# A Conformer block on one core: token tiles of 127 rows in place of 125

## Chip, core and metric

The kernel runs on 1 core of one Trainium2 chip. The metric is the device time of one execution in microseconds (us), the median of several runs. The profile is of one execution; its span runs from the first to the last instruction and is 3.8 to 4.3 us shorter than the time of the same run. All runs told here are in the fast state, with a mean granted TensorE clock of 0.998 to 1.000 of full speed.

## The reference, cut to what matters

Two batches of 4000 tokens with 512 features; a feed-forward, full attention inside each batch, a convolution block, a second feed-forward.

```python
B, T, D, K = (2, 4000, 512, 3);  F = 4 * D
h = _silu(layernorm(x) @ w_ff1_a) @ w_ff1_b              # FF1
x1 = x + 0.5 * h
q, k, v = (layernorm(x1) @ w for w in (w_q, w_k, w_v))
p = softmax(q @ k.T * scale)                             # 4000 x 4000 for each batch
x2 = x1 + (p @ v) @ w_o
a, b = split(layernorm(x2) @ w_pw1)                      # pointwise product 1
h = a * sigmoid(b);  dc = depthwise_conv(h, dw)          # 3 taps along the tokens
h = _silu(batchnorm(dc)) @ w_pw2                         # pointwise product 2
x3 = x2 + h
h = _silu(layernorm(x3) @ w_ff2_a) @ w_ff2_b             # FF2
return layernorm(x3 + 0.5 * h)
```

## The kernel before

Tokens sit in tiles of 125 rows, 64 tiles for 8000 tokens, and are worked on in 16 chunks of 4 tiles, 500 tokens:

```python
TILE = 125
CHUNK = 500
TPC = CHUNK // TILE
NT = N // TILE           # 64
NCK = N // CHUNK         # 16 chunks
TCB = T // CHUNK         # 8 chunks of a batch
KT = -(-T // 128)        # 32 key tiles of a batch
```

In the first half of a feed-forward the weights are the stationary operand and the tokens stream; in the second half a token tile is stationary and 512 features stream, whatever the number of its rows:

```python
def ff_first(self, c, f, p, b_p):
    ...
    for cc in range(0 if done else DC):
        self.mm(out, self.Wa[:, cc, f * 128:(f + 1) * 128], self.lnT[c % 2][:, :, cc, 0:TILE], ...)
    self.act(p, ps[:, 0:CHUNK], AF.Silu, [b_ps], [b_p])

def ff_second(self, f, ti, p, b_p, inc):
    self.mm(self.Yb[ti][0:TILE, :], p[:, ti * TILE:(ti + 1) * TILE], self.Wb[:, f, :], ...)
```

Attention takes one chunk of queries `g` after the other, and in it 32 key blocks `kt` (4 score and 4 value matmuls each). Beside the blocks, other work is put in: queries of the next chunk are fetched (blocks 7 to 10) and multiplied (14 to 20), the pointwise product of the chunk before runs (`pair`, at blocks 22 and 27), and in chunk 7 the keys of batch 1 replace those of batch 0, one key tile for each block from block 6 on:

```python
if g + 1 < NCK and 7 <= kt < 7 + TPC:
    self.fetch_queries((g + 1) // TCB, (g + 1) % TCB, kt - 7)
if g + 1 < NCK and kt in (14, 16, 18, 20):
    self.q_group((g + 1) // TCB, (g + 1) % TCB, (kt - 14) // 2)
if not self.any_score:
    if g == TCB - 1 and kt >= 6:
        self.key_tile(1, kt - 6)
    if g == TCB and kt < 6:
        self.key_tile(1, KT - 6 + kt)
hook(g, kt)              # kt 22, 27: pair(g - 1, ...); kt 3, 8: pair(g - 2, ...)
```

A key tile is two transfers, and both are issued by SyncE (SP), which also issues all the other transposes, stores and loads of this stage (the times are those of SP's timeline in the profile before, at 952.93 and 953.56 us):

```python
def key_tile(self, b, kt):
    ...
    self.load(self.h[kt], src, [self.b_h[kt]], reads=rd)                 # on SP: 0.58 us of its queue
    self.transpose(self.hT[kc][:, kj], src, rd, [self.b_hT[kc][kj]])     # on SP: 1.19 us of its queue
```

SP's timeline shows its transfers one after the other, none begun before the one ahead was done (from 930.13 to 962.67 us, 32.54 us, in the profile before), so what stands behind a key tile in SP's order waits for it.

## Time and profile before

| | kernel before |
|---|---|
| time, median of 3 (lowest to highest) | 2054.76 us (2054.47 to 2054.98) |
| span of the profiled run | 2050.2 us |
| TensorE (PE) busy | 2037.8 us, 99% |
| VectorE (DVE), ScalarE (ACT), GpSimd (POOL) busy | 54%, 36%, 5% |
| second halves of the feed-forwards | 2016 matmuls of 125 rows x 512 columns |

The lines behind the table stand in the prediction. PE is the bound and has next to no gaps, so only two things move the time: fewer or shorter matmuls, and waits of PE. In the list of waits of the SP queue in the stretch of attention chunk 7 (from 928 to 968 us; columns: who waits, for whom, us in all, times, longest) the first row is:

```profile
SPq L529 <- DVE wff L1030: 3.3, 1, 3.3
```

SP (its queue is shown as SPq) stood still once for 3.3 us, for a piece of the convolution on VectorE whose result it stores. The store began at 930.13 us, when VectorE was done, and what stands behind it from 930.49 on; neither was set by TensorE.

### The profile page before, as it was taken

The page shows a single profiled execution, that of the slowest core. Times are in us where ns is not written, and L with a number is a line of the kernel's source. Part 1 is how long each engine was busy: PE and PEld are TensorE (multiplying, and loading weights), DVE is VectorE, ACT ScalarE, POOL GpSimd, SP SyncE. Part 2 cuts the span into 40 slices and gives each one's busy share as a digit, 9 for nine tenths or more (in the row PEclk, how much of TensorE's full clock was granted, in tenths as well). Part 3 has the DMA queues.
Part 4 walks back from the last instruction along what each step waited for, and adds up shares of the span by engine and source line. Part 5 has one row for each costly group of instructions (what it writes and reads, how often), then busy time and mean ns, then how long its engine had stood idle before and what let it go on. Part 6 is the DMA issues. An engine that isn't in the chain of part 4 may idle for free.

```text
span 2050.2 us, 24503 instructions
## 1 busy us (share of the span) xinstructions
PE 2037.8 (99%) x9653; PEld 1031.8 (50%) x9653; DVE 1099.0 (54%) x2274; ACT 742.7 (36%) x1270; POOL 112.2 (5%) x241
## 2 busy tenths in 40 slices
PE   9999999999999999999999999999999999999998
PEld 5555555554444444444444444444445555555554
DVE  4234444325556667666666676667764543543443
ACT  3433333333333333333333333333345343443432
POOL 1000000000000000000000000000011000000000
PEclk9999999999999999999999999999999999999999
DMA  7122256420101111115411110111143111111111
GB/s 184 51 61 61 53 103 125 90 69 16 26 16 30 25 29 26 34 23 116 107 27 24 29 34 24 24 29 34 47 120 93 31 34 39 31 33 39 31 31 42
DMA packets 253417, 104.60 MB, mean 51 GB/s; under 512 B 193703, under 2 KB 252784, under 8 KB 253296
## 3 DMA queue, kind: packets, MB, share of 16 engines
q1 hardware_dynamic: 252900, 102.65, 21.4%
q8 instruction: 78, 1.28, 0.3%
q14 instruction: 43, 0.35, 0.1%
q10 hardware_dynamic: 396, 0.31, 0.0%
HBM read 33.73 MB, written 23.31 MB: 28 GB/s over the span
## 4 chain that ended last, share of the span: by engine, by line
PE 98%; DVE 1%; POOL 0%; issue 0%; ACT 0%; DMA 0%; POOLq 0%; SPq 0%; DVEq 0%; ACTq 0%
PE s L470 55%; PE y L470 42%; DVE work L552 0%; POOL work L672 0%; DVE work L574 0%; DVE wff L1092 0%; DVE xt L695 0%; DMA xt<-in_x_dram 0%; DVE work L509 0%; POOL work L1101 0%; DVE work L665 0%; ACT work L512 0%; DVE wff L997 0%; DVE work L618 0%; DVE work L670 0%
## 5 line engine op out<-in xcount | busy, mean ns | idle before, releaser
L512 ACT ACTIVATE work<-s 128x500 bf16<-128x500 f32 (+1 forms) x1060 | 621.6, 587 | 1218.0 <-PE s L470 1216.6
L470 PE MATMUL s<-work,wff 128*128 128x500 bf16 (+2 forms) x2592 | 628.5, 373 | 1.9 <-DVE work L509 1.7
L470 PE MATMUL s<-work,keys 128*128 128x500 bf16 x2048 | 517.5, 374 | 0.1
L470 PE MATMUL y<-wff,work 128*125 128x512 bf16 x2016 | 506.6, 379 | 0.0
L470 PE MATMUL y<-work,keys 128*128 128x500 bf16 (+1 forms) x2048 | 504.6, 374 | 0.4 <-DVE work L929 0.4
L854 DVE TENSOR_TENSOR work<-work 128x500 f32<-128x500 f32 (+1 forms) x496 | 334.4, 674 | 280.0 <-ACT work L512 277.2
L470 PEld LDWEIGHTS s<-work,wff 128*128 128x128 bf16 x2592 | 250.6, 98 | 279.8 <-issue 5.8
L470 PEld LDWEIGHTS y<-wff,work 128*125 128x125 bf16 x2016 | 275.2, 137 | 173.5
L470 PEld LDWEIGHTS s<-work,keys 128*128 128x128 bf16 x2048 | 199.8, 98 | 232.2 <-DVE work L778 0.6
L470 PEld LDWEIGHTS y<-work,keys 128*128 128x128 bf16 (+1 forms) x2048 | 194.6, 97 | 234.0 <-issue 6.2
L695 DVE SCALAR_TENSOR_TENSOR xt<-y,xt 125x512 bf16<-125x512 f32 x128 | 79.8, 683 | 353.0 <-PE y L470 353.0
L552 DVE BATCH_NORM_STATS2 work<-xt 125x6 f32<-125x512 bf16 x316 | 199.7, 680 | 8.3 <-DMA xt<-in_x_dram 8.1
L470 PE MATMUL s<-work 128*125 128x512 bf16 (+2 forms) x780 | 197.7, 378 | 2.0 <-DVE work L1202 1.2
L561 POOL TENSOR_TENSOR work<-work 125x4 f32<-125x4 f32 x76 | 77.0, 1013 | 1131.5 <-DVE work L559 1131.5
L470 PEld LDWEIGHTS s<-work 128*125 128x125 bf16 (+1 forms) x780 | 95.3, 124 | 76.9 <-issue 3.7
L574 DVE TENSOR_SCALAR work<-xt,work 125x512 bf16<-125x512 bf16 x311 | 113.9, 412 | 26.3 <-POOL work L561 22.5
L695 DVE SCALAR_TENSOR_TENSOR xt<-s,xt 125x512 bf16<-125x512 f32 x56 | 38.7, 691 | 146.4 <-PE s L470 146.4
L695 DVE SCALAR_TENSOR_TENSOR xt<-s,work,xt 125x512 bf16<-125x512 f32 x64 | 48.0, 751 | 32.2 <-PE s L470 31.5
L1001 DVE SCALAR_TENSOR_TENSOR wff<-wff,s 128x500 bf16<-128x500 f32 x57 | 38.5, 676 | 40.8 <-PE s L470 40.8
L512 ACT ACTIVATE wff<-s 128x500 f32<-128x500 f32 x67 | 39.5, 591 | 54.8 <-PE s L470 54.8
L512 ACT ACTIVATE work<-keys,work 128x500 bf16<-128x500 bf16 x64 | 50.5, 796 | 1.1 <-DVE work L1106 1.1
L1071 POOL COPY wff<-wff 128x1 bf16<-128x1 bf16 x56 | 10.5, 187 | 635.4 <-DVE wff L1001 633.0
(83 smaller groups left out, 429.6 us busy)
## 6 DMA issues: line engine op xcount, KB each, us to landing
keys<-keysd SPq DMA_DIRECT2D x62, 128.0 KB, 2.3
xt<-in_x_dram SPq DMA_DIRECT2D x15, 500.0 KB
out_dram<-work SPq DMA_DIRECT2D x15, 500.0 KB
dcvd<-wff SPq DMA_DIRECT2D x52, 125.0 KB, 1.7
keys<-dcvd SPq DMA_DIRECT2D x13, 500.0 KB, 5.1
keysd<-work SPq DMA_DIRECT2D x16, 320.0 KB, 3.2
wff<-in_w_ff_a_dram SPq DMA_DIRECT2D x16, 256.0 KB, 3.9
work<-work SPq DMA_TRANSPOSE x210, 2.5
```

What stands on the lines that cost most here:

```text
L470: self.S.op("PE", lambda e: e.matmul(out, lhsT, rhs, start=start, stop=stop, **kw), reads=reads, writes=[bank], inc=stop if inc is None el ...
L512: return self.S.op("ACT", lambda e: e.activation(out, in_, func, **kw), reads=reads, writes=writes)
L552: self.S.op("DVE", lambda e: e.bn_stats(self.st[sl][:, ti, :], x), reads=[b_x], writes=[self.b_st[sl][ti]])
L561: S.op("POOL", lambda e: e.tensor_tensor(out=self.rs[sl], in0=self.va[sl], in1=self.neghalf[0:TILE, :], op=ALU.pow), reads=self.b_va[sl] + ...
L574: self.S.op("DVE", lambda e: e.tensor_scalar(out, x, self.mv[sl][:, ti, 0:1], self.rs[sl][:, ti:ti + 1], ALU.subtract, ALU.mult), reads=[b ...
L695: self.S.op("DVE", lambda e: e.scalar_tensor_tensor(out=self.XT[g], in0=ps, scalar=scalar, in1=self.XT[g], op0=ALU.mult, op1=ALU.add), rea ...
L854: S.op("DVE", lambda e, p=p, n=n, acc=acc: e.tensor_tensor(out=acc, in0=acc, in1=self.P[p][0:n], op=ALU.add), reads=[self.b_P[p], self.b_a ...
L1001: self.S.op("DVE", lambda e: e.scalar_tensor_tensor(out=out, in0=self.th[k], scalar=1.0, in1=ps[:, 0:CHUNK], op0=ALU.add, op1=ALU.mult), r ...
L1071: S.op("POOL", lambda e: e.tensor_copy(self.G[gs][:, jj, 0:1], self.G[gp][:, jj, CHUNK:CHUNK + 1]), reads=[self.b_G[gp][jj]], writes=[self ...
```

## The change

The intent is to fill the tiles better: 4000 = 31 x 127 + 63, so a batch takes 31 full tiles and a rest of 63 tokens. The rests of both batches share one tile (rows 0 to 62 and 64 to 126). That is 63 tiles in place of 64. A chunk has 508 tokens, the last one of each batch 444, of which the last 63 are in the shared tile.

```diff
-TILE = 125
-CHUNK = 500
-TPC = CHUNK // TILE
-NT = N // TILE
-NCK = N // CHUNK
-TCB = T // CHUNK
+TILE = 127
+TPC = 4
+CHUNK = TPC * TILE
+TCB = -(-T // CHUNK)
+NCK = B * TCB
+TAIL = T % TILE
+NT = NCK * TPC - 1
+SHARED = TCB * TPC - 1
+HALF = 64
...
+def width(c):
+    return CHUNK if c % TCB < TCB - 1 else T - (TCB - 1) * CHUNK      # 508, or 444
+def token_tiles(c):
+    return TPC if c < NCK - 1 else TPC - 1
+def tile_at(c, ti):
+    return SHARED if c == NCK - 1 and ti == TPC - 1 else c * TPC + ti
...
-    ROWS = ((0, 80), (80, TILE))
+    ROWS = ((0, 112), (112, TILE))
...
 # ff_first, ff_second: n = token_tiles(c) tiles, the last chunk has 3
-                for ti in range(TPC):
-                    self.ff_second(f, ti, self.P[s], self.b_P[s], f == FC - 1 or ti == TPC - 1)
+                n = token_tiles(c)
+                for ti in range(n):
+                    self.ff_second(f, ti, self.P[s], self.b_P[s], f == FC - 1 or ti == n - 1)
...
 # attention: chunks of width W
-                    self.mm(ps[:, 0:CHUNK], self.hT[kc][:, kj, cc, :], self.qT[s][:, cc, :],
+                    self.mm(ps[:, 0:W], self.hT[kc][:, kj, cc, :], self.qT[s][:, cc, 0:W],
...
 # pointwise product 1: the short chunk of batch 0 in two pieces, 381 and 63 columns
+            if n < TPC:
+                moves.append((ps[:, n * TILE:W], self.lnT[0][:, n, :, tile_rows(t, n)]))
...
 # loads and stores of a chunk in pieces of 112 and 15 rows (load_x before: one transfer of 125 rows)
+            res += [(rows[r0:r1], tiles[r0:r1, lo:min(hi, n), :]) for r0, r1 in self.ROWS]
```

The order of the instructions on the SP queue and the blocks to which key tiles, queries and pointwise products are tied stay as they were.

## The prediction

A weight load took 98 ns with 128 columns and 137 with 125, both less than the 211 and 216 ns from one matmul to the next. The "2.4" in the sums is the step from 211 to 216 ns over 12 columns, 2.4 columns for each ns.

> **What bounds the kernel now.** I read the page's busy times and its chain first, then the groups of matmuls by form, then timelines of one feed-forward and one attention stretch, and last the DMA-issuing queue (SPq) in attention chunk 7. From the page:
>
> ```profile
> span 2050.2 us, 24503 instructions
> ...
> PE 2037.8 (99%) x9653; PEld 1031.8 (50%) x9653; DVE 1099.0 (54%) x2274; ACT 742.7 (36%) x1270; POOL 112.2 (5%) x241
> ...
> PE 98%; DVE 1%; POOL 0%; issue 0%; ACT 0%; DMA 0%; POOLq 0%; SPq 0%; DVEq 0%; ACTq 0%
> ```
>
> TensorE is busy for all but 12.4 us of the span, and the chain that ended last is 98% matmuls. No other engine is above 54%. So the time is the sum of matmul pitches (start to next start), plus 12.4 us of gaps: about 2.8 us in the head, 3.5 where attention ends, 5.5 after the last matmul. A changed instruction on DVE, ACT or POOL is worth nothing except there. The groups, one row for each form:
>
> ```profile
> L470 PE MATMUL y<-wff,work 128*125 128x512 bf16 x2016 | 506.6, 379 | 0.0
> ...
> L470 PEld LDWEIGHTS s<-work,wff 128*128 128x128 bf16 x2592 | 250.6, 98 | 279.8 <-issue 5.8
> L470 PEld LDWEIGHTS y<-wff,work 128*125 128x125 bf16 x2016 | 275.2, 137 | 173.5
> ```
>
> The first row is the second half of both feed-forwards: a token tile of 125 rows is the stationary operand, 512 features stream past. Its length is 512 whatever the tile's rows. The mean of 379 ns is a latency, not a pitch (2016 x 379 exceeds the group's busy time), so the pitch is read from starts, in the timeline of PE:
>
> ```profile
> 218.56 1.89 PE L470 MATMUL y<-wff,work 128*125 128x512 bf16 x8
> 220.29 1.01 PE L470 MATMUL s<-work,wff 128*128 128x500 bf16 x4
> ...
> 831.91 1.00 PE L470 MATMUL y<-work,keys 128*128 128x500 bf16 x4
> 832.75 1.01 PE L470 MATMUL s<-work,keys 128*128 128x500 bf16 x4
> 833.60 1.00 PE L470 MATMUL y<-work,keys 128*128 128x500 bf16 x4
> ```
>
> Eight of 512 columns take 220.29 - 218.56 = 1.73 us, 216 ns each. Eight of 500 take 833.60 - 831.91 = 1.69 us, 211 ns each. A matmul is paid by the columns it streams, about 0.4 ns each, plus about 3 ns.
>
> [...]
>
> **The change part by part.** I counted matmuls and streamed columns of both built programs (the part that runs): 9652 and 4,816,721 before, 9648 and 4,798,121 after.
>
> Removed: one token tile of 64. Each feed-forward loses 16 matmuls of 512 columns, the second pointwise product 4. That is 36 x 216 ns = 7.8 us, all on PE, so all on the path.
>
> Unchanged: the first halves of the feed-forwards, scores, values, queries and first pointwise product stream the same 4000 tokens per batch. Matmuls of 508 cost 3.3 ns more than those of 500, those of 444 and 381 (last chunk of a batch) less; the sum of columns there differs by only -168, below 0.1 us. The projections stay at 64 groups of 4, because a shared tile is projected once for each batch.
>
> Added on PE: for chunk 7 each group of the first pointwise product is split into 381 + 63 columns: 8 groups x 4 = 32 more matmuls of 63 columns with a full weight load. In the head, 16 matmuls of 125 columns start at 7.92 us and the next work at 9.00, or 68 ns each, and 16 weight loads of 128x128 take 0.92 us, or 57 ns each. I take 57 ns for a 63-column one. The pair 381 + 63 then costs 162 + 57 = 219 ns against 188 in one piece: 31 ns x 32 = 1.0 us.
>
> Moved, and the part where I had to choose: attention chunks 7 and 15 are only 444 wide. A key block (4 score and 4 value matmuls) falls from 1.69 to 1.69 - 8 x 56 / 2.4 ns = 1.50 us. In chunk 7 of the kernel before, the SP queue brings in the other batch's keys, and it is full:
>
> ```profile
> 952.93 0.58 SPq L516 DMA_DIRECT2D keys<-keysd  x1
> 953.56 1.19 SPq L520 DMA_TRANSPOSE keys<-keysd  x1
> 954.85 3.33 SPq L520 DMA_TRANSPOSE work<-work  x2
> 958.23 0.57 SPq L516 DMA_DIRECT2D keys<-keysd  x1
> 958.86 1.20 SPq L520 DMA_TRANSPOSE keys<-keysd  x1
> 960.15 2.52 SPq L520 DMA_TRANSPOSE work<-work  x2
> ```
>
> One key tile costs the queue 0.58 + 1.19 us and two gaps, 1.85 us, and behind them stand the four transposes that the pointwise product at key block 22 reads. The last is issued at about 961.4 and lands about 2.6 us later, at 964.0. The chain shows the product there with a small wait of its own, against the same place one chunk earlier:
>
> ```profile
> 896.88 2.55 PE s L470 x12
> ...
> 964.22 2.62 PE s L470 x12
> ```
>
> Slack there is nil (0.07 us waited). Afterwards PE arrives 22 x 0.187 = 4.1 us earlier, less 0.1 for the 508-wide pieces between. The queue's 32.5 us from 930.13 to 962.67 do not shrink: it starts when a store of about block 7 is ready, 7 x 0.187 = 1.3 us earlier, and one gap of 0.4 us (947.22 to 947.60) can close. PE then waits 0.07 + 4.0 - 1.7 = 2.4 us; I take 2.2. Nothing gives this back, as PE is the bound. In chunk 15 the transposes for block 22 are issued from 1491.35, the last at 1496.0 with 2.9 us to landing, so 1498.9, and PE needs them at 1499.53: 0.6 us of slack. The 5.5 blocks from the normalisation to there shrink by 1.0 us: a wait of about 0.5 us.
>
> Where attention ends, a chain of VectorE work runs, part of it on the last chunk, now 444 wide in place of 500. Four gates and four statistics of 0.68 us lose about 0.07 us each: 0.4 us less, allowing for two split copies.
>
> Sum: -7.8 + 1.0 + 2.2 + 0.5 - 0.4 = -4.5 us. On 2054.76 that is 2050.3 us, 0.2% faster.
>
> **Rivals.** (1) The full gain: the SP queue speeds up with PE, because what gates it are key tiles released by PE, and no wait appears. For it: the wait list of that stretch shows a few SPq waits on PE. Against: from 947.60 on the queue's pieces stand nearly end to end. Then -7.8 + 1.0 - 0.4 = -7.2: 2047.6 us. (2) A larger wait: the transposes are slowed further by the queue's long pieces (one took 2.03 us in place of 1.2), or the next query fetch in chunk 8 is late too (its slack before is about 1.9 us, after about 0.7 to 1.5), or chunk 15, where VectorE is 78% busy, becomes bound by VectorE for a few blocks. Then waits of 5 to 6 us eat most of the gain: 2053 us. (3) The transfers of 112 + 15 rows or the doubled count of issues hurt head or end. Against: outside attention SP is mostly idle, and head and end move one tile each as before; at most 0.3 us either way. (4) A weight load of 127 columns shows at the 381-wide matmuls of the short chunk (162 ns): 137 ns still fits; at most some tenths.
>
> **Range and chances.** The 7.8 us are nearly certain, the 1.0 within 0.5 us; the waits of 2.7 us may be 0 to 6. Runs before lie within 0.5 us. So 2050.3, with 2047.6 to 2052.8 for 8 in 10. A change of 2% is 41 us, far outside all of it: faster by over 2% 0.005, within 2% 0.985, slower by over 2% 0.01.
>
> **What would show it.** Groups: 1992 + 24 matmuls of 127 rows with 512 columns, each still at 216 ns pitch, weight loads at about 137 ns. A feed-forward chunk at 27.4 us before should be about 27.6 (508 wide), and the last about 20.9. The 63-column pieces at about 57 ns. PE idle for about 2 us just before block 22 of chunk 7, released by a DMA transpose, with SPq full before it, and about 0.5 us in chunk 15. Wrong would be: PE's pitch of 508 above 215 ns, no idle in chunk 7 (then rival 1), idle of more than 4 us there, or a gap at a new place.

## The result, and the profile after

| | before | after |
|---|---|---|
| time, median (lowest to highest) | 2054.61 us (2054.38 to 2054.98), 4 runs | 2053.22 us (2051.23 to 2054.26), 4 runs |
| ratio of the fast runs, 95% interval | | 0.9992 (0.9975 to 1.0009) |
| span of the profiled run | 2050.2 us | 2047.4 us |

A ratio here is the mean time of one kernel's fast runs over that of the other's of the same rounds, so it is not quite the ratio of the medians beside it. The prediction of 2050.3 us was 2.9 us too low, and the result lies 0.4 us above the range. Two things stand out: the gain is 1.4 us at the median in place of 4.5, and the runs spread over 3.0 us where those before spread over 0.6. The profiled run of the changed kernel is its fastest one (2051.23 us), so its profile alone cannot explain the median.

From the page after, the span, the busy times and the chain:

```profile
span 2047.4 us, 24513 instructions
...
PE 2029.9 (99%) x9647; PEld 1028.7 (50%) x9649; DVE 1092.7 (53%) x2264; ACT 744.9 (36%) x1274; POOL 109.7 (5%) x236
...
PE 97%; DVE 1%; DMA 0%; SPq 0%; issue 0%; POOL 0%; ACT 0%; POOLq 0%; DVEq 0%; ACTq 0%
```

PE is busy for 2037.8 - 2029.9 = 7.9 us less, but the span is only 2.8 us shorter: some 5 us came back as waits of PE. DMA and SPq now stand ahead of issue in the chain. The groups (line, engine, operation, operands, partitions x elements, count; busy us, mean ns; idle before) show the change itself:

```profile
L500 PE MATMUL y<-wff,work 128*127 128x512 bf16 x1992 | 501.2, 379 | 0.0
...
L500 PEld LDWEIGHTS y<-wff,work 128*127 128x127 bf16 x1992 | 273.7, 137 | 171.4
```

There are 24 fewer matmuls in this group, at the same latency, and a weight load of 127 columns takes 137 ns as one of 125 did. Where the time went is seen by stages. The limits were read from both chains of work and PE timelines (times from the span's start):

| stage | before, us | after, us | difference |
|---|---|---|---|
| head, up to the first second-half matmul | 14.11 | 14.51 | +0.40 |
| FF1, up to the first query product | 440.05 | 436.97 | -3.08 |
| attention | 1064.98 | 1068.97 | +3.99 |
| transition to FF2 | 38.48 | 38.48 | 0.00 |
| FF2, up to its last tile | 483.68 | 479.36 | -4.32 |
| end | 8.9 | 9.1 | +0.2 |

The feed-forwards give what they should (another 0.4 us of FF1's share falls after the first query product, and so into attention). Attention takes nearly all of it back, and most of that at one place. From the timeline of PE after (start, us, instructions, the idle time before them and what ended it):

```profile
962.56 0.91 PE L500 MATMUL y<-work,keys 128*128 128x444 bf16 x4
966.97 1.89 PE L500 MATMUL s<-work,wff 128*128 128x508 bf16 x8 [3.50 <-issue]
```

These eight are the pointwise product at key block 22 of chunk 7, the place the prediction named. "issue" hides the cause: the last semaphore event that the profile shows was long past when PE started. The chain through this stretch (start, us, what) shows what PE followed:

```profile
963.03 2.44 DMA work<-work
965.47 1.50 issue
966.97 2.64 PE s L500 x12
```

A transpose into the operand (`work<-work`) began at 963.03 and was done after 2.44 us; another transpose was issued right behind it, and PE started 1.50 us after the first had landed. The SP queue's timeline shows those two and what they stood behind:

```profile
958.18 2.89 SPq L558 DMA_TRANSPOSE work<-work  x2
961.12 0.57 SPq L554 DMA_DIRECT2D keys<-keysd  x1
961.74 1.19 SPq L558 DMA_TRANSPOSE keys<-keysd  x1
963.03 2.52 SPq L558 DMA_TRANSPOSE work<-work  x2
```

The transposes that PE needs are issued at 958.18 and 963.03, without a pause, with a key tile's two transfers between them. SP was done with the last at 965.55; before, it was done at 962.67. PE reached block 22 at 964.07 then and at 963.31 now. And as before, this queue was let go by VectorE:

```profile
SPq L567 <- DVE wff L1112: 3.2, 1, 3.2
```

The wait of 3.5 us explains the profiled run. A second profile of the same kernel, below, explains a part of the spread.

### The profile page after: what moved, and what is told of

Its sections match the earlier page's. It is cut to its first block, busy times and chain, and to the rows that moved or that the text cites. A ratio compares the mean times of both kernels' runs of the same rounds, so it can differ in the third digit from the quotient of the medians.

```text
span 2047.4 us, 24513 instructions
## 1 busy us (share of the span) xinstructions
PE 2029.9 (99%) x9647; PEld 1028.7 (50%) x9649; DVE 1092.7 (53%) x2264; ACT 744.9 (36%) x1274; POOL 109.7 (5%) x236
## 4 chain that ended last, share of the span: by engine, by line
PE 97%; DVE 1%; DMA 0%; SPq 0%; issue 0%; POOL 0%; ACT 0%; POOLq 0%; DVEq 0%; ACTq 0%
PE s L500 55%; PE y L500 42%; DVE wff L1176 0%; SPq L558 0%; DVE work L612 0%; DMA work<-work 0%; DMA wff<-in_w_ff_a_dram 0%; DVE xt L753 0%; SPq L562 0%; DVE work L634 0%; POOL work L726 0%; POOL work L1185 0%; ACT work L550 0%; DVE work L547 0%; SPq L554 0%
## 5 line engine op out<-in xcount | busy, mean ns | idle before, releaser
L550 ACT ACTIVATE work<-s 128x508 bf16<-128x508 f32 (+3 forms) x1060 | 622.8, 588 | 1211.9 <-PE s L500 1208.3
L500 PE MATMUL s<-work,wff 128*128 128x508 bf16 (+5 forms) x2624 | 628.3, 371 | 6.4 <-issue 3.5
L500 PE MATMUL s<-work,keys 128*128 128x508 bf16 (+1 forms) x2048 | 516.8, 374 | 0.1
L500 PE MATMUL y<-work,keys 128*128 128x508 bf16 (+2 forms) x2048 | 504.2, 373 | 0.4 <-DVE work L999 0.4
L500 PE MATMUL y<-wff,work 128*127 128x512 bf16 x1992 | 501.2, 379 | 0.0
L920 DVE TENSOR_TENSOR work<-work 128x508 f32<-128x508 f32 (+2 forms) x496 | 334.5, 674 | 279.8 <-ACT work L550 278.6
L500 PEld LDWEIGHTS y<-wff,work 128*127 128x127 bf16 x1992 | 273.7, 137 | 171.4
L612 DVE BATCH_NORM_STATS2 work<-xt 127x6 f32<-127x512 bf16 x312 | 197.2, 680 | 5.9 <-DMA xt<-in_x_dram 5.8
L500 PE MATMUL s<-work 128*127 128x512 bf16 (+3 forms) x776 | 197.0, 378 | 2.2 <-DVE work L1292 1.2
L634 DVE TENSOR_SCALAR work<-xt,work 127x512 bf16<-127x512 bf16 x307 | 110.7, 406 | 26.2 <-POOL work L621 23.0
```

Of the source, the lines that this page charges most:

```text
L500: self.S.op("PE", lambda e: e.matmul(out, lhsT, rhs, start=start, stop=stop, **kw), reads=reads, writes=[bank], inc=stop if inc is None el ...
L550: return self.S.op("ACT", lambda e: e.activation(out, in_, func, **kw), reads=reads, writes=writes)
L612: self.S.op("DVE", lambda e: e.bn_stats(self.st[sl][:, ti, :], x), reads=[b_x], writes=[self.b_st[sl][ti]])
L634: self.S.op("DVE", lambda e: e.tensor_scalar(out, x, self.mv[sl][:, ti, 0:1], self.rs[sl][:, ti:ti + 1], ALU.subtract, ALU.mult), reads=[b ...
L920: S.op("DVE", lambda e, p=p, n=n, acc=acc: e.tensor_tensor(out=acc, in0=acc, in1=self.P[p][0:n, 0:W], op=ALU.add), reads=[self.b_P[p], sel ...
```

## The experiments

Two theories stood against each other. The clock theory (A in the texts): the gain is lost in the wait before block 22, and in the slower runs a second time, because the wait lets TensorE's granted clock fall. The rival: the wait costs what it lasts, and the spread comes from elsewhere (a wait whose length varies, the pieces of the transfers, the head). All kernels ran with 5 rounds beside the kernel before on the same chip, and all gave the right result. The medians of the kernel before were 2054.45 us (2054.09 to 2055.09) on the chip of the first batch, 2054.32 (2053.58 to 2055.87) on that of the second and 2054.49 (2054.30 to 2056.72) on that of the third; the mean clocks told are those of the records. These are nine runs each, so the kernel before itself spreads over 1.0, 2.3 and 2.4 us, more than the 0.6 of the four runs above.

### e0_after: the changed kernel again

No edit.

> The changed kernel again, to see its spread and the span and clock of each run. Theory A[...]: the runs spread over 2051 to 2054.5 us, and longer runs show a lower mean granted clock. Rival B (the spread was the state of that chip, nothing of the kernel): on this chip the runs lie within 0.6 us as those of the kernel before do, near 2051.2.

Measured: 2053.25 us (2051.70 to 2054.03), ratio 0.9991 (0.9978 to 1.0005). The profile fell on a run of 2053.85 us and shows what the first did not. From PE's timeline:

```profile
966.81 3.55 PE L500 MATMUL s<-work,wff 128*128 128x508 bf16 x8 [3.81 <-issue]
```

The same eight matmuls take 3.55 us in place of 1.89. The table of stretches (us, then busy time of PE, PEld, DVE, ACT, POOL, then the granted clock PEclk, DMA share, GB/s) has the reason, first in the fast profile of the changed kernel, then in this one:

```profile
963.00:967.00 4.00, 0.50 (x4) 0.09 (x3) 0.62 (x1) 0.30 (x1) 0.00 (x0) 1.00 0.50 102
967.00:970.00 3.00, 3.00 (x15) 1.43 (x16) 0.69 (x1) 0.95 (x2) 0.28 (x2) 1.00 0.64 156
```

```profile
963.00:967.00 4.00, 0.19 (x1) 0.14 (x2) 0.48 (x1) 0.00 (x0) 0.00 (x0) 0.80 0.53 111
967.00:970.00 3.00, 3.00 (x8) 1.04 (x7) 0.00 (x0) 0.59 (x1) 0.00 (x0) 0.50 0.63 157
970.00:974.00 4.00, 4.00 (x16) 1.77 (x15) 1.31 (x2) 0.90 (x2) 0.30 (x2) 0.72 0.54 132
```

PEclk is the third number from the right: 1.00 throughout in the one, 0.80, 0.50 and 0.72 in the other, with 8 matmuls in 3 us in place of 15. From the start of the product, 16 matmuls take 972.69 - 966.81 = 5.88 us here and 970.19 - 966.97 = 3.22 in the fast profile: the drop costs 2.66 us more. The two spans, 2050.0 and 2047.4 us, differ by 2.6. So one part of the spread is this: about the same wait, with or without a clock drop after it. The first four runs line up with that: 2051.23 us at a mean clock of 1.000, 2052.75 and 2053.68 at 0.999, 2054.26 at 0.998. The five of this batch don't: 2051.91 us has 0.998, as 2054.03 has. The third digit is a coarse witness, because the clock also falls after the last matmul, where it costs nothing (in e1_keys_act that alone, 0.82 over the last 9 us and 1.00 in all stretches before, gives 0.999). A mean of 1.000 leaves no room for a drop of 3.4 us, the shortest one seen (half of it over 2050 us is 0.0008), but a mean of 0.999 can be with or without one.

How long such a drop lasts, the traces show when they are read in stretches of 0.2 us (here the drop's first and last one and the fall after the last matmul, then that fall in the first profile after):

```profile
965.40:965.60 0.20, 0.00 (x0) 0.00 (x0) 0.00 (x0) 0.00 (x0) 0.00 (x0) 0.54 0.95 196
972.20:972.40 0.20, 0.20 (x3) 0.09 (x1) 0.00 (x0) 0.20 (x1) 0.00 (x0) 0.89 0.85 138
2047.40:2047.60 0.20, 0.00 (x0) 0.00 (x0) 0.00 (x0) 0.00 (x0) 0.00 (x0) 0.61 0.00 0
...
2046.80:2047.00 0.20, 0.00 (x0) 0.00 (x0) 0.00 (x0) 0.00 (x0) 0.00 (x0) 0.97 0.12 41
```

The share below 1.00 places each edge inside its stretch: the clock is at half from 965.42 to 972.24 us, for 6.83 us. Read in the same way from stretches of 2 us, it is so for 6.8 us in e8_before_delay and for 3.4 us in e3_pause1 (below): the first two are twice the third. The profiles before and after show one more length, in the trace's clock records: in both these begin with 2041.17 us at full clock (from 5.81 and 5.82 us), until 2046.98 and 2046.99 us, though the last matmul had ended at 2044.74 in the one and at 2041.73 in the other. So in these two the fall does not come at a fixed distance from the end of the work.

An estimate from these lengths is that the clock changes only at the edges of a fixed period of 3.4133 us: the 2041.17 us are 598 of it, the 6.83 us are 2, and from the start of the drop to that of the fall at the end (2047.44) are 1082.03 us here, which is 317. If so, the edges can be placed in each run. The periods that ended in a drop held 2.42 us of idle PE here, 2.9 in e8_before_delay and 2.16 in e3_pause1. In the first profile after, the fall at the end (2046.99) less 317 periods puts an edge at 964.96: it cuts the wait of 3.50 us into 1.49 and 2.01, and the clock stayed. By this estimate, that is why much the same wait is followed by a drop in one run and not in another. These few periods are too few to give a threshold.

### e1_keys_act: the key loads of batch 1 issued by ScalarE

```diff
-        self.load(self.h[kt], src, [self.b_h[kt]], reads=rd)
+        self.load(self.h[kt], src, [self.b_h[kt]], "ACT" if b else "SP", reads=rd)
```

It takes 0.58 us for each key tile off SP's queue and leaves bytes, order and buffers as they are. Only the plain load moves; all transposes stay on SP.

> The changed kernel with the plain loads of batch 1's key tiles issued by the ACT queue in place of SP; the transposes stay on SP. SP then pays about 1.25 us for a key tile in place of 1.85 and keeps up with blocks of 1.5 us. Theory A (the SP queue is what holds the transposes back): the idle time of 3.5 us before block 22 of chunk 7 is gone (below 0.3 us), so 2051.2 - 3.5 = 2047.7 us, and all runs within 0.6 us[...]. Rival C (the transposes themselves or the DMA engines are slow there, whoever issues): the wait stays at 2 us or more, 2050 us or above.

Measured: 2048.05 us (2047.34 to 2048.35), ratio 0.9967 (0.9954 to 0.9981), 6.4 us below the kernel before and 5.2 below the changed one on the same chip, all clocks 0.999 or 1.000. PE's timeline:

```profile
962.48 0.91 PE L500 MATMUL y<-work,keys 128*128 128x444 bf16 x4
963.42 1.89 PE L500 MATMUL s<-work,wff 128*128 128x508 bf16 x8
```

and the queue's:

```profile
957.70 3.63 SPq L558 DMA_TRANSPOSE work<-work  x2
```

SP is done with the last transpose at 957.70 + 3.63 = 961.33 us, 4.2 earlier than in the changed kernel, and PE starts the product at 963.42 without a wait listed. The difference per stage against the kernel before is head +0.3, FF1 -3.1, attention +0.5, FF2 -4.3, end +0.35: the 7.8 us less the small costs. The spread is 1.0 us, as that of the kernel before on this chip; 0.6 was expected. Both theories have the wait as the main cost, and it is: its end removes 5.2 us at the median, which is more than its 3.5 to 3.8 us.

### e5_before_keys_act: the same edit on the kernel before

The same diff, applied to the kernel before.

> The kernel before with the same move of the key loads to the ACT queue, as a control: its wait at that place was 0.07 us, so both theories expect the time of the kernel before, 2054.6, less 0.1, within 0.3 us. More than 0.5 us off would say that the ACT queue's issues cost or save something of their own, and the gain of the run above would not be the wait alone.

Measured: 2054.57 us (2054.48 to 2054.94), ratio 1.0001 (0.9987 to 1.0015). Where PE waited for 0.07 us only, a faster queue is worth nothing. So the gain of e1_keys_act is not one that this edit would give to any version; it undoes a cost of the change.

### e2_fill: matmuls of no use in the wait

```diff
+    def fill(self, n):
+        r = self.rings.get("S", 0) % 4
+        ps, b_ps = self.Sb[r], self.b_S[r]
+        for k in range(n):
+            self.mm(ps[:, 0:444], self.hT[5][:, 0, k % DC, :], self.qT[1][:, k % DC, 0:444], True, True,
+                    [self.b_hT[5][0], self.b_qT[1][k % DC]], b_ps, inc=k == n - 1)
...
+            if g == TCB - 1 and kt == 22 and not any_score:
+                self.fill(15)
```

The 15 matmuls stand just before the product and take 15 x 188 ns = 2.8 us of the wait. The bank that they write is overwritten by the product. This keeps PE busy without shortening anything, so it tells the clock from the wait.

> The changed kernel with 15 useless score matmuls of 444 columns (15 x 0.188 = 2.8 us) put into the wait before block 22 of chunk 7; the queue is as slow as before, so the wait stays as long, but TensorE is busy for most of it. Theory A: the time is that of the best run of the changed kernel, 2051.2 us (+0.3), and the spread of its runs falls below 0.8 us with the clock at 0.999 to 1.0. Rival B: the spread stays as in the changed kernel, up to 2054. If the filler does not fit into the wait the time rises by up to 2.8 us over 2051.2.

Measured: 2052.39 us (2051.35 to 2052.58), ratio 0.999 (0.9976 to 1.0003), clocks 1.000 in four runs and 0.999 in one. PE's timeline of it:

```profile
963.03 2.98 PE L500 MATMUL s<-work,keys 128*128 128x444 bf16 x15
967.04 1.89 PE L500 MATMUL s<-work,wff 128*128 128x508 bf16 x8 [1.03 <-DMA work<-work]
```

One us of wait is left, the product takes 1.89 us again, and PEclk is 1.00 in all stretches around it. No run is at 2053 or above. The profile fell on the fastest run, but a mean clock of 1.000 excludes a drop in three of the others too. So the clock drop hangs on PE's idle time, not on the transfers, and is gone where PE is kept busy. But the median is 1.2 us above what was expected, and the spread of 1.2 us was to be below 0.8. The median of the changed kernel fell by only 0.9 us. And the runs at 1.000 still spread from 2051.35 to 2052.58 us, so about 1 us of the spread is not the clock. It is perhaps the length of the wait; the runs without a profile don't show it. This stays open.

### e8_before_delay: the wait made in the kernel before

```diff
                     if g == TCB - 1 and kt >= 6:
                         self.key_tile(1, kt - 6)
+                    if g == TCB - 1 and kt == 15:
+                        for k in range(2):
+                            self.key_tile(1, k)
```

Two key tiles are loaded a second time, which puts 2 x 1.85 us on SP's queue ahead of the transposes; nothing of the change is in it.

> The kernel before (tiles of 125 rows) with two key tiles loaded a second time at block 15 of chunk 7: 3.7 us more work for SP ahead of the transposes, nothing else. It tests the queue's arithmetic and the clock without the change. Queue alone: a wait of 0.07 + 3.7 = 3.8 us before block 22, so 2054.5 + 3.7 = 2058.2 us in all runs, spread about 1 us. Queue and clock (theory A): the same wait, and in some runs up to 2.6 us more: 2058.2 to 2060.8, the long ones with a lower mean clock. If SP had slack there the time rises by less than 3 us.

Measured: 2059.55 us (2057.50 to 2061.25), ratio 1.0024 (1.001 to 1.0038), 5.2 us above the kernel before at the median. PE's timeline and two of the stretches behind the wait (columns as above):

```profile
967.54 3.49 PE L470 MATMUL s<-work,wff 128*128 128x500 bf16 x8 [3.70 <-DMA work<-work]
```

```profile
968.00:970.00 2.00, 2.00 (x7) 0.66 (x6) 0.00 (x0) 0.59 (x1) 0.00 (x0) 0.50 0.54 131
970.00:972.00 2.00, 2.00 (x6) 0.74 (x5) 0.68 (x1) 0.00 (x0) 0.11 (x1) 0.50 0.57 142
```

The wait is 3.70 us, two key tiles of the queue almost to the digit, and the clock is at half behind it; here the releaser is named as the transpose. From the product's start 20 matmuls take 974.70 - 967.54 = 7.16 us, against 968.37 - 964.14 = 4.23 in the kernel before: the drop costs 2.9 us. Wait and drop, 6.6 us, are about what the span grew by (2056.5 - 2050.2 = 6.3 us). Tiles of 127 rows are not needed for any of it. A late transpose at this place is enough, and that a wait costs only its length does not hold in this run. The five runs spread over 3.75 us; the fastest, 2057.50, is even 0.7 us below what the wait alone was expected to give.

### e3_pause1: no key tile at one block

```diff
-                    if g == TCB - 1 and kt >= 6:
+                    if g == TCB - 1 and 6 <= kt < 14:
                         self.key_tile(1, kt - 6)
-                    if g == TCB and kt < 6:
-                        self.key_tile(1, KT - 6 + kt)
+                    if g == TCB - 1 and kt >= 15:
+                        self.key_tile(1, kt - 7)
+                    if g == TCB and kt < 7:
+                        self.key_tile(1, KT - 7 + kt)
```

> The changed kernel, but block 14 of chunk 7 brings in no key tile, and all later ones come one block later, so one key tile (1.85 us of SP) moves from before the four transposes to after them. Theory A (queue, and clock after a long wait): the wait before block 22 falls from 3.5 to 3.8 us to 1.7 to 2.0[...]; the time is 2051.2 to 2051.7 (the changed kernel's runs that kept their clock) less 1.85, 2049.3 to 2050.0 us, with a spread of about 1 us as in the kernel before. Rival B (spread not due to the wait): median 2053.2 - 1.85 = 2051.4, spread of 2 us and more.

Measured: 2050.94 us (2050.48 to 2051.57), ratio 0.9982 (0.9969 to 0.9996). From PE's timeline:

```profile
965.50 3.00 PE L500 MATMUL s<-work,wff 128*128 128x508 bf16 x8 [2.16 <-issue]
```

The wait is down by 1.34 us, less than the 1.85 of a key tile. The estimate had been that so short a wait brings no clock drop. That was wrong: the eight matmuls take 3.00 us, PEclk is 0.53 and 0.62 in the two stretches from 966 to 970, and 16 matmuls take 4.90 us in place of 3.22. That drop of 1.7 us belongs to the profiled run, the slowest (2051.57 us, clock 0.998). The runs of 2050.48 and 2050.94 us (the median) have a mean of 1.000 and so no such drop, and still lie 0.5 to 0.9 us above the expectation; up to 0.5 of it is the wait, 2.16 us in place of 1.7 to 2.0, and the rest stays open. So a wait of 2.16 us was followed by half clock here (0.53), and one of 3.50 us by full clock (1.00) in the first profile after.

### e4_pause2: no key tile at two blocks

As e3_pause1, with `kt >= 16`, `kt - 8`, `kt < 8` and `KT - 8`.

> The same with two blocks left out: two key tiles, 3.7 us of SP, behind the transposes. Theory A: the wait is 0 to 0.3 us and the time that of the run with the loads on the ACT queue, 2048.0 us (within 0.5), though nothing has left SP; only the order changed. Rival D (the ACT version gains by something else than the wait): 2049 us or more. A new wait in chunk 8, where the query transposes now come up to 3.7 us later, would show as idle time before its block 14, up to 2 us.

Measured: 2051.57 us (2049.59 to 2052.40), ratio 0.9982 (0.9969 to 0.9996). PE's timeline at both places:

```profile
963.75 1.89 PE L500 MATMUL s<-work,wff 128*128 128x508 bf16 x8 [0.81 <-issue]
...
1015.20 1.02 PE L500 MATMUL s<-work 128*128 128x508 bf16 x4 [2.23 <-DMA work<-keysd]
1016.06 1.69 PE L500 MATMUL s<-work,keys 128*128 128x508 bf16 x4
```

Block 22 of chunk 7 now waits for only 0.81 us. But the two tiles put off to chunk 8 stand ahead of its query fetches there, and the query product waits for 2.23 us, with slow matmuls behind it (4 in 1.48 us from start to start, in place of 0.86). SP works without a pause there until the transposes of the queries are issued (1013.5 us). This order moved the wait on; less work on SP took it away.

### e7_best and e9_x_mid: e1_keys_act, and the head

The head had become 0.4 us longer. The head's timeline of PE in the changed kernel shows where:

```profile
9.33 0.62 PE L500 MATMUL s<-work,wff 128*128 128x127 bf16 x8 [0.61 <-DMA wff<-in_w_ff_a_dram]
```

PE waits for a slice of the first weights. The 16 loads of weights in the head land in 7.0 us at the median, in place of 5.5. In between stands the load of chunk 1's tokens, now in pieces of 112 and 15 rows, where it was one transfer of 125 rows. That the pieces hold up the weights was the estimate. Both kernels put that load behind more of the weights, e7_best behind all of them, e9_x_mid behind slice 5:

```diff
-            if k == 3:
+            if k == self.NWA - 1:      # e9_x_mid: k == 5
                 self.load_x(1)
```

> The key loads of batch 1 on the ACT queue, and chunk 1's tokens loaded after all weights of the first feed-forward in place of after half of them. In the changed kernel these tokens come in pieces of 112 and 15 rows and the next weight slice landed late (TensorE waited 0.3 to 0.6 us for it in the head, 0 to 0.2 before). If the two compete for the DMA engines, the wait for weights in the head goes and the time is 2048.05 - 0.4 = 2047.6 us; if not, 2048.0 within 0.3.

Measured: 2049.27 us (2047.18 to 2053.74), ratio 0.9982 (0.9968 to 0.9995). The wait for the weights is gone, but the tokens land 6 us later, SP's next jobs slip, and the taps of the convolution come late. PE's timeline:

```profile
47.83 0.25 PE L500 MATMUL s<-work 3*128 3x3 bf16 x4 [1.83 <-DMA work<-in_dw_dram]
```

A wait of 1.83 us in place of one of 0.6, and a spread of 6.6 us (2047.18 to 2053.74), which one profile (of 2049.05) does not explain: a failure.

> The same, with chunk 1's tokens loaded after the sixth of eight weight slices, in place of after the fourth or (as failed before) after all: the tokens should arrive about 3 us later than in the changed kernel, not 6, early enough for the convolution taps not to wait in the SP queue, and the wait for weights in the head (0.3 to 0.6 us) should shrink. Competition for the DMA engines: 0.2 to 0.5 us below the run beside it, no wait of TensorE for the taps. Otherwise the same time, or the wait for the taps again (over 1 us slower).

Measured: 2047.64 us (2047.00 to 2048.08), ratio 0.9964 (0.9951 to 0.9978). Neither the wait for the taps nor a gain: the wait for the weights was still 0.44 us. The times to landing speak for the token load: 5.3 to 5.5 us at the median in the three profiles with tiles of 125 rows, 6.5 to 7.5 with 127 and the old order, 6.2 in e9_x_mid and 5.6 in e7_best. But the start of the first second-half matmul varies from run to run by as much as is at stake: 13.72, 14.11 and 14.19 us in those three profiles, 13.97 to 14.51 in the seven with 127 rows and the old order. e5_before_keys_act too waited 0.4 us for a slice. So the 0.4 us of the head are those of one pair of profiles; what the change costs there is not clear from these runs.

### e10_keys_act_again: e1_keys_act on another chip

No edit against e1_keys_act; it ran beside e9_x_mid.

> The changed kernel with batch 1's key loads on the ACT queue once more, on another chip than the first time. If its gain is the wait and the clock's part of it, it repeats: before less 6.4 us (within 0.6), spread about 1 us, no run with the clock halved in chunk 7. If the first result was that chip's state, the difference is below 5 us here.

Measured: 2047.55 us (2047.27 to 2048.37), ratio 0.9965 (0.9951 to 0.9979), 6.9 us below the kernel before. The gain holds. In its profile PE did wait at block 22, for 0.68 us where e1_keys_act's list has no wait, without a clock drop. So the length of that wait varies by 0.6 us or more between two runs of one kernel, which fits what e2_fill left open but doesn't prove it. This is the best version: it beats both kernels, by 0.35% the one before.

## Why the prediction was wrong

- **Removed matmuls, -7.8 us: right.** PE's busy time fell by 7.9 us; the stages gave 4.3 in FF2 and 3.1 in FF1, with 0.4 more inside attention. e1_keys_act gets nearly all of it.
- **63-column pieces, +1.0 us: mis-sized, 0.1.** The term "I take 57 ns for a 63-column one" was too high. The 16 matmuls of such a product after take 1.54 us from start to start; less 8 x 162 ns for the 381-wide ones (56 of these in a row take 9.09 us, from 2022.11 to 2031.20) that leaves 30 ns each. The 57 ns in the head are explained by the stream itself: there 16 matmuls of 127 columns take 0.90 us from start to start after (10.01 to 10.91), 56 ns each. Together with 216 ns for 512 columns that is 0.42 ns for each column and 3 ns more, which gives 55 ns for 125 columns and 29 for 63. So the 57 ns were no bound set by weight loads; the 63-column pieces have weight loads too.
- **Wait before block 22 of chunk 7, +2.2 us: the mechanism was right, the size was not, 3.5.** It failed at "it starts when a store of about block 7 is ready, 7 x 0.187 = 1.3 us earlier, and one gap of 0.4 us (947.22 to 947.60) can close". From the pointwise product at key block 3 of the chunk (921.67 before, 924.44 after) PE reached block 22 3.53 us sooner, as predicted (19 x 0.187 = 3.55). But the store came only 0.28 us sooner (8.46 and 8.18 us behind that product) where the prediction has 4 x 0.187 = 0.75 from there, because it waits for VectorE. And from the store to the last transpose the queue took 32.93 us in place of 32.54, where 0.4 less were expected: the gap closed, and other pieces grew (one transpose took 1.87 us). 0.07 + 3.53 - 0.28 + 0.39 = 3.7 us, against 3.5 listed (3.66 from the expected start to the real one). The queue's pieces are the larger part of the miss, 0.8 us, the store the smaller, 0.5.
- **What the wait does to the clock: not in the sum, and most of what lifts the median out of the range.** Every rival took a wait to cost its length. In the profile of e0_after it cost 2.66 us more, and e8_before_delay and e3_pause1 show the same (2.9 and 1.7). Kept busy in e2_fill, with a clock of 1.000 in four runs of five, PE gave 2051.35 to 2052.58 us, all inside the range. The median is 2.0 us above the run of the profile without a drop; how much of that is the clock and how much the wait's own variation was not separated to better than about 1 us.
- **Chunk 15, +0.5 us: right.** PE waited for 0.4 us there for a transpose.
- **End of attention, -0.4 us: no gain.** The transition takes 38.48 us in both kernels. The shorter VectorE pieces do stand on its chain (0.62 us in place of 0.68 for a gate), but PE's two longest waits for ScalarE there grew from 0.96 and 0.84 to 1.12 and 1.03 us; what made these longer was not taken apart.
- **Not foreseen, about +0.8 us together in the profiled pair:** the head +0.4 us (within the variation from run to run, see e9_x_mid); the end +0.2; and the projection of the shared tile inside attention, whose 4 matmuls with 63 columns of weights end 0.2 us later than their pitch of 216 ns would have it (the next matmul starts at 1010.87 us).

The sum of what was found is -7.8 + 0.1 + 3.5 + 0.4 + 0.8 = -3.0 us for a run without a clock drop; the span shows -2.8. The rival nearest to the truth was the second, a larger wait, with 2053 us. The first of its three reasons holds in part: a transpose of the queue took 1.87 us in place of 1.19. The waits that it expected in chunk 8 and from VectorE in chunk 15 did not come. There is one wait of 3.5 us, and in some runs a clock drop.

## What to carry to other kernels

Where one engine is busy 99% of the time, look for what stands on a full DMA queue behind it: making that engine's work shorter in front of a transfer that cannot come earlier gives it back as waiting (here PE came 3.53 us sooner and waited for 3.5 us), and one line that moves a second kind of transfer to another queue was worth more (5.2 us) than the change had given (1.4 us), and worth nothing without the change. Ask for each queue what lets it start, and whether that thing gets faster too. And a wait on TensorE of the lengths seen here has to be priced with the matmuls after it, not only with its length: behind waits of 2.16, 3.70 and 3.81 us they ran at half the clock (0.50 to 0.53) and took 1.7, 2.9 and 2.7 us more, and behind one of 3.50 us they did not. A profile of one run may show that or not, so profile a second one where the times of the runs spread.
